# Signs of the expert weights on GpSimd, a new first-block order and an earlier far block in an attention and two-MLP kernel

## The chip, the cores and the metric

One core of one Trainium2 chip runs one launch. The metric is the device time in microseconds; before the change the median of three runs was 943.58 us (941.25 to 945.59).

## The reference, cut to what matters

Inputs are f32 (the weights reach the chip as 64-bit words, see below). Attention has 4 batches, 8 heads, 576 positions and head size 64. Heads 0 to 3 look back over 32 positions, heads 4 to 7 at positions of the same residue modulo 32. Then two MLPs over 2304 tokens follow:

```python
attn = softmax(where(mask, q @ k.T / 8, -1e9)) @ v      # per head
x = attn as (2304, 512)
h = x @ w_in;  x = (h - tanh(h)) @ w_out                # d_ff 2048
xn = x / sqrt(mean(x * x) + 1e-6) * rms_g
out = (silu(xn @ w_gate) * (xn @ w_val)) @ w_out        # d_ff 1536
```

## The kernel before, in words

Tokens are cut into nine sub-blocks of 256 (`subs`, numbered 0 to 8) and these into five groups, (0,1), (2,3), (4), (5,6), (7,8); group 2 is half as wide. The first MLP runs group by group, and in a group over 16 slices f of d_ff: `pe_h` makes h in 12 matmuls (three products of high and low fp32r parts, four chunks of 128), ScalarE takes the tanh (L680), VectorE subtracts and splits the result (L685, L696) with a ScalarE cast (L691) between, and `pe_x` adds 12 matmuls into four banks. The second MLP (from about 480 us) is TensorE work alone as far as the time goes.

A weight tile comes as 64-bit floats, 128 x 512 of them. `Weight.scale` (ScalarE L165, for the first five tiles GpSimd L167) scales the upper words into `ca`; `Weight.merge` builds the f32 on VectorE in three steps: L174 shifts `ca` left by three into `ct`, L175 puts the sign bit of `ca` in, L178 puts the top three bits of the lower words in. ScalarE casts to the high part (L185) and VectorE subtracts for the low part (L189). The 32 tiles of the first MLP are made this way while group 0 runs, two per slice f; the 36 tiles of the second MLP follow in the last group.

Attention of a sub-block is one `Local` object and, for the strided heads, a `Dense` one (sub-blocks 0 to 3, "near", and 6, "far") or `Strided` ones (4, 5, 7, 8). Local and Dense have four steps: `s` (score matmuls, then on VectorE the row maxima L298 or L301, on ScalarE the exp L312, on VectorE the sums and the scaling L320 to L322), `p` (TensorE transposes L331, ScalarE copies L335), `v` (matmuls with v) and the write-out to `xs` (L338, L342). Strided products are made by GpSimd (L504 for q and k, L537 for the probabilities and v) and reduced by VectorE (L509, L544).

What sets the order: the first block is written out by hand in the string `START` (s0L is step `s` of Local 0, m, e, n are its maxima, exp and scaling, A scale on GpSimd, B merge, P and Q the two parts, h a `pe_h`). After it a planner orders every engine's instructions, except that TensorE keeps the written order from group 1 on. During group g the attention of group g+1 is issued: `STINT[g]` lists the slices f before which its next s, p or v step is put (`pe_work`), and `work` spreads the strided items over slices. `EARLY = (5,)`: sub-block 5's strided scores are made in group 1 already.

Of the kernel before, what the change touches and what calls it, by code (L numbers as in the profile page):

```python
# [7 lines left out]
F32 = mybir.dt.float32  # L8
# [5 lines left out]
ALU = mybir.AluOpType  # L14
# [9 lines left out]
START = """  # L24
<tabcdwABwCDwww2ww
W9
s0Lx m0L0 s0Dx m0L1 m0D0 e0L0 m0D1 e0L1 n0L0 p0L0h0 A0 e0D0 n0L1 B0 p0L1h1 c0L0a s1Lx c0L1a e0D1 n0D0 v0Lh0
P0 n0D1 p0D0m0 y0L0 A1 p0D1m1 y0L1 z0L0 c0D0a z0L1 s1Dx c0D1a Q0 v0Dh1 m1L0 m1L1 y0D0 y0D1 z0D0 A2 e1L0 z0D1
m1D0 h0h0 e1L1 n1L0 m1D1 p1L0m0 T0 G0 c1L0a n1L1 I0 e1D0 J0 p1L1m1 B1 c1L1a e1D1 n1D0 P1 n1D1 p1D0m0 Q1
c1D0a p1D1m1 B2 v1Lm0 A3 c1D1a v1Dm1 y1L0 y1L1 z1L0 P2 h1h1 z1L1 y1D0 Q2 y1D1 z1D0 A4 X0 T1 z1D1 G1 h2h0 B3  # L30
# [5 lines left out]
def attn_moe_moe_kernel(  # L36
# [24 lines left out]
    nc = tc.nc  # L61
# [12 lines left out]
    groups = [(0, 1), (2, 3), (4,), (5, 6), (7, 8)]  # L74
    width = [SUB * len(g) for g in groups]
    NG = len(groups)
# [3 lines left out]
    def runs(s):  # L80

        r = []
        for i, (b, t) in enumerate(subs[s]):
            if r and r[-1][0] == b and r[-1][1] + r[-1][2] == t:
                r[-1][2] += 64
            else:
                r.append([b, t, 64, 64 * i])
        return r
# [3 lines left out]
    NEAR = 4  # L92

    SOON = {2: 6, 3: 2}
    STINT = {1: (5, 8, 11), 2: (1, 3, 4, 5, 7, 8, 10, 11, 13), 3: (1, 3, 5, 8, 10, 12)}
    GC = 2
    PR = 5 * 64
    LANES = (5, 7, 8)
    EARLY = (5,)
# [21 lines left out]
    for s in range(len(subs)):  # L121
        if len(runs(s)) > 1 or s in LANES:
            _, t0, n, _ = runs(s)[0]
# [25 lines left out]
    class Weight:  # L149
        def __init__(self, kind, f):  # L150
            self.kind, self.f = kind, f

        def load(self):
            kind, f = self.kind, self.f
            r = wts.tile([128, 4, 128], w_in.dtype, tag="w", name="raw")
            self.raw = r
            src = {"in": w_in, "gate": w_gate, "val": w_val, "out": w_out, "out2": w_out2}[kind]
            nc.sync.dma_start(out=r.rearrange("p c f -> p (c f)"), in_=src[f])

        def scale(self, eng):  # L160
            w = self.raw.rearrange("p c f -> p (c f)").bitcast(U32).rearrange("p (n t) -> p n t", t=2)
            self.lo, hi = w[:, :, 0], w[:, :, 1]
            self.a = cvt.tile([128, 512], F32, tag="ca", name="ca")
            if eng is nc.scalar:
                nc.scalar.mul(out=self.a, in_=hi.bitcast(F32), mul=2.0 ** -111)  # L165
            else:
                nc.gpsimd.tensor_scalar(  # L167
                    out=self.a, in0=hi.bitcast(F32), scalar1=2.0 ** -111, scalar2=1.0, op0=ALU.mult, op1=ALU.mult
                )

        def merge(self):
            a = self.a.bitcast(U32)
            t = cvt.tile([128, 512], U32, tag="ct", name="ct")
            nc.vector.tensor_scalar(out=t, in0=a, scalar1=3, scalar2=None, op0=ALU.logical_shift_left)  # L174
            nc.vector.scalar_tensor_tensor(  # L175
                out=t, in0=a, scalar=0x80000000, in1=t, op0=ALU.bitwise_and, op1=ALU.bitwise_or
            )
            nc.vector.scalar_tensor_tensor(  # L178
                out=t, in0=self.lo, scalar=29, in1=t, op0=ALU.logical_shift_right, op1=ALU.bitwise_or
            )  # L180
            self.b = t.bitcast(F32)
# [71 lines left out]
    class Heads:  # L253
# [35 lines left out]
        def st_m(self, i):  # L289

            w, ps = self.w, self.ps
            self.sm[i] = sm = self.room("sm", i, 4 * w).rearrange("q (h p t) -> q h p t", h=2, p=2)
            self.nm[i] = nm = att.tile([128, 2, 2], F32, tag="nm", name="nm", bufs=4)
            self.ss[i] = att.tile([128, 2, 2], F32, tag="ss", name="ss", bufs=4)
            m = dmask if w == 128 else mask if not self.near else add[96][:, i] if w == 96 else add[64]
            for hh in range(2):
                if self.early:
                    nc.vector.tensor_reduce(out=nm[:, hh], in_=ps[hh][:, i], axis=AX.X, op=ALU.max)  # L298
                else:
                    for p in range(2):  # L300
# [47 lines left out]
    class Local(Heads):  # L348
        w = 96
# [237 lines left out]
    loc = [Local(j) for j in range(len(subs))]  # L587
# [9 lines left out]
    class Work:  # L597


        def __init__(self, js):  # L600
            self.pe, self.st = [], []
            for j in js:
                kinds = [loc[j]]
                if isinstance(strd[j][0], Dense):
                    kinds += strd[j]
                else:
                    for o in strd[j]:
                        self.st += o.pvs if j in EARLY else o.items().qks + o.pvs
                    if j + 1 == EARLY[0]:
                        for o in (strd[i][0] for i in EARLY):  # L610
                            self.st += o.items().qks
                for nm, k in zip("spsvpv", (0, 0, 1, 0, 1, 1)):
                    if k < len(kinds):
                        self.pe.append(lambda o=kinds[k], nm=nm: self.stage(o, nm))

        @staticmethod
        def stage(o, nm):
# [42 lines left out]
    def new_x(g):  # L660
        if g < NG:
            xs[g] = mid.tile([128, 2, 4, 512], F32R, tag="xs", name="xs")
            for k, j in enumerate(groups[g]):
                xh[j] = xs[g][:, :, :, SUB * k:SUB * k + SUB]
# [182 lines left out]
    wks = [Work(groups[1])]  # L847
# [78 lines left out]
    for g, f, a, e in units:  # L926
        if g == 0:
            st1.to(2 * (f + 4))
        elif f == 0:
            if g == 1:  # L930
                order = ctx.enter_context(ExitStack())
                order.enter_context(tc.manual_schedule(engines={mybir.EngineType.PE}))
            if g == NG - 1:
                order.close()
            assert not wks[-1].pe and not wks[-1].st
            new_x(g + 1)
            if g + 1 < NG:
                wks.append(Work(groups[g + 1]))
        if g == NG - 1 and f == 0:
            poolT.close()  # L940
            pbx = ctx.enter_context(tc.tile_pool(name="pbx", bufs=1, side="right", reuse_waits="tile"))
            gcol = pbx.tile([128, 4], F32, name="gcol")
            nc.sync.dma_start(out=gcol, in_=rms_g.rearrange("(c p) -> p c", p=128))
            ones = pbx.tile([128, 128], F32R, name="ones")
            nc.vector.memset(ones.bitcast(F32), 1.0)
        rem = FA - 1 - f
        wk = wks[-1]

        def pe_work():
            if g in STINT:  # L950
                wk.run_pe(len(wk.pe) if f in STINT[g] else 0)
            elif f >= 2:
                wk.run_pe(max(rem, 1))

        def work():
            if f >= 6 or 0 < g < NG - 1:
                wk.run(wk.st, max(rem - SOON.get(g, 0), 1))

        unit(g, f, a, e, pe_work, work)
        if g == NG - 1:  # L960
            if f == 4:
                pg = prep(0, pbx)
            if pg is not None:
                next(pg, None)
# [127 lines left out]
```

## Time and profile before

| | us |
|---|---|
| median of the runs | 943.58 |
| the profiled execution | 945.39 |
| its span | 943.7 |
| TensorE busy | 911.2 |
| VectorE busy | 571.0 |
| ScalarE busy | 345.0 |
| GpSimd busy | 159.9 |

The span runs from the first to the last instruction; 1.7 us of the execution's time lie outside it. A view of stretches gives each engine's busy time and the granted TensorE clock in each, as a share of full speed. An instruction's row gives its start, its duration, and in brackets how long its engine had been idle and what ended that.

### The profile page before, as it was taken

The numbers are of one execution on the slowest core, as the hardware profiler recorded it, in microseconds if no ns is written. First come the engines' busy times: TensorE is split into PE (matmuls) and PEld (weight loads), VectorE is DVE, ScalarE is ACT, GpSimd is POOL, SyncE is SP. The second block draws the span as 40 slices with busy tenths as digits, with TensorE's granted clock in tenths as the row PEclk, the third lists the DMA queues.
The fourth block names the chain that finished last, engine by engine and source line by source line (L and its number), as shares of the span: only waits on it lengthen the run. The fifth ranks groups of instructions, "written<-read, shape, count | busy, mean of one in ns | idle before, by whom it ended". The sixth has DMA issues, their size and how long they took to land.

```text
span 943.7 us, 13656 instructions
## 1 busy us (share of the span) xinstructions
PE 911.2 (97%) x5251; PEld 756.8 (80%) x5251; DVE 571.0 (61%) x1263; ACT 345.0 (37%) x795; POOL 159.9 (17%) x216
## 2 busy tenths in 40 slices
PE   6799998999899999999999999999999999999998
PEld 4677876888799787888888888888888888888897
DVE  4899998987748979359999682262125312421212
ACT  4776743322453424256566332222111211111211
POOL 0100136784408686000000000000000000000000
PEclk8799998999999999999999999999999999999999
DMA  9845433311222110066444210101010001000100
GB/s 289 268 168 185 143 93 97 103 56 51 91 75 75 49 38 1 1 223 194 164 155 140 86 49 19 45 3 43 0 45 1 23 1 44 1 1 1 45 1 23
DMA packets 33729, 72.86 MB, mean 77 GB/s; under 512 B 6976, under 2 KB 15552, under 8 KB 33664
## 3 DMA queue, kind: packets, MB, share of 16 engines
q1 hardware_dynamic: 33664, 71.99, 23.5%
q8 instruction: 41, 0.67, 0.3%
q14 instruction: 24, 0.20, 0.1%
HBM read 62.54 MB, written 9.44 MB: 76 GB/s over the span
## 4 chain that ended last, share of the span: by engine, by line
PE 61%; DVE 2%; issue 0%; POOL 0%; DVEq 0%
PE ps_x L145 23%; PE ps_h L145 22%; PE ps_m L145 16%; DVE so L544 1%; DVE sm L301 0%; DVE g L696 0%; DVE tg L685 0%; PE ps_v L145 0%; DVE sm L322 0%; POOL pr L504 0%; DVE os L820 0%; POOL pr L537 0%; PE ps_p L331 0%; DVE pr L552 0%; DVE xs L563 0%
## 5 line engine op out<-in xcount | busy, mean ns | idle before, releaser
L145 PE MATMUL ps_x<-g,w 128*128 128x512 f32 (+1 forms) x984 | 221.0, 373 | 4.0 <-DVE w L189 2.1
L145 PE MATMUL ps_h<-xs,w 128*128 128x512 f32 (+1 forms) x984 | 214.4, 366 | 1.0 <-DVE xs L342 0.8
L145 PEld LDWEIGHTS ps_x<-g,w 128*128 128x128 f32 x984 | 171.3, 193 | 36.5 <-DVE w L189 3.0
L145 PEld LDWEIGHTS ps_h<-xs,w 128*128 128x128 f32 x984 | 170.6, 190 | 31.2 <-DVE xs L342 0.9
L795 DVE SCALAR_TENSOR_TENSOR s<-ps_m,s 128x512 f32<-128x512 f32 (+1 forms) x60 | 38.3, 638 | 222.9 <-PE ps_m L145 222.8
L145 PE MATMUL ps_h<-xn,w 128*128 128x512 f32 (+1 forms) x720 | 159.0, 369 | 0.0
L145 PE MATMUL ps_m<-xn,w 128*128 128x512 f32 (+1 forms) x720 | 158.4, 368 | 0.0
L145 PE MATMUL ps_x<-w,p 128*128 128x512 f32 x648 | 157.8, 391 | 0.0
L145 PEld LDWEIGHTS ps_h<-xn,w 128*128 128x128 f32 x720 | 126.8, 188 | 24.5
L145 PEld LDWEIGHTS ps_m<-xn,w 128*128 128x128 f32 x720 | 125.9, 188 | 23.1
L145 PEld LDWEIGHTS ps_x<-w,p 128*128 128x128 f32 x648 | 120.7, 188 | 25.6
L504 POOL TENSOR_TENSOR pr<-sk,sq 128x256 f32<-128x256 f32 (+2 forms) x101 | 83.1, 857 | 119.8 <-DMA sk<-in_k_str_dram 78.9
L794 ACT ACTIVATE s<-ps_h 128x512 f32<-128x512 f32 (+1 forms) x60 | 33.4, 556 | 163.9 <-PE ps_h L145 163.6
L537 POOL TENSOR_TENSOR pr<-sv,se 128x288 f32<-128x288 f32 (+12 forms) x104 | 72.0, 713 | 64.0 <-DVE so L544 19.7
L797 ACT CAST p<-s 128x512 fp32r<-128x512 f32 (+1 forms) x60 | 34.6, 577 | 122.4 <-DVE s L795 122.3
L691 ACT CAST g<-tg 128x512 fp32r<-128x512 f32 (+1 forms) x82 | 46.5, 568 | 86.2 <-DVE tg L685 85.7
L685 DVE SCALAR_TENSOR_TENSOR tg<-ps_h,tg 128x512 f32<-128x512 f32 (+1 forms) x82 | 50.6, 617 | 34.5 <-ACT tg L680 34.3
L680 ACT ACTIVATE tg<-ps_h 128x512 f32<-128x512 f32 (+1 forms) x82 | 44.4, 542 | 70.8 <-PE ps_h L145 70.4
L544 DVE TENSOR_REDUCE so<-pr 128x16 f32<-128x240 f32 (+11 forms) x104 | 64.3, 650 | 6.3 <-POOL pr L537 5.8
L696 DVE TENSOR_TENSOR g<-tg,g 128x512 fp32r<-128x512 f32 (+1 forms) x82 | 55.0, 670 | 10.2 <-ACT g L691 9.9
L798 DVE TENSOR_TENSOR p<-s,p 128x512 fp32r<-128x512 f32 (+1 forms) x60 | 38.2, 637 | 25.8 <-ACT p L797 25.6
L165 ACT ACTIVATE ca<-raw 128x512 f32<-128x512 f32 x63 | 41.9, 672 | 28.0 <-issue 8.0
(79 smaller groups left out, 674.6 us busy)
## 6 DMA issues: line engine op xcount, KB each, us to landing
raw<-in_w_out_dram SPq DMA_DIRECT2D x28, 512.0 KB, 5.2
raw<-in_w_in_dram SPq DMA_DIRECT2D x16, 512.0 KB, 7.8
raw<-in_w_gate_dram SPq DMA_DIRECT2D x12, 512.0 KB, 3.9
raw<-in_w_val_dram SPq DMA_DIRECT2D x12, 512.0 KB, 4.2
x2d<-xe SPq DMA_DIRECT2D x36, 128.0 KB, 1.8
x<-x2d SPq DMA_DIRECT2D x16, 256.0 KB, 3.9
out_dram<-o SPq DMA_DIRECT2D x16, 256.0 KB, 2.0
sk<-in_k_str_dram SPq DMA_DIRECT2D x4, 576.0 KB, 3.8
```

The source lines that it names most:

```text
L145: nc.tensor.matmul(out_, lhsT, rhs, start=start, stop=stop, skip_group_check=True)
L165: nc.scalar.mul(out=self.a, in_=hi.bitcast(F32), mul=2.0 ** -111)
L504: nc.gpsimd.tensor_tensor(out=pr, in0=self.k[:, a:e, :], in1=self.q[:, c - c0:c - c0 + 1, :].to_broadcast([128, e - a, D]), op=ALU.mult,)
L537: nc.gpsimd.tensor_tensor(out=pr, in0=self.v[:, 0:c + 1, a:e], in1=self.e[:, c - c0, 0:c + 1].unsqueeze(2).to_broadcast([128, c + 1, e - a ...
L544: pend.append(lambda: nc.vector.tensor_reduce(out=o[:, c - g0, a:e], in_=pr.rearrange("l c d -> l d c"), axis=AX.X, op=ALU.add))
L680: nc.scalar.activation(out=t, in_=h_of[g, f, a], func=ACTF.Tanh, scale=WS)
L685: nc.vector.scalar_tensor_tensor(out=t, in0=h_of.pop((g, f, a)), scalar=WS, in1=t, op0=ALU.mult, op1=ALU.subtract)
L691: nc.scalar.copy(out=t[:, 0], in_=t_of[g, f, a])
L696: nc.vector.tensor_tensor(out=t[:, 1], in0=t_of.pop((g, f, a)), in1=t[:, 0].bitcast(F32), op=ALU.subtract)
L795: nc.vector.scalar_tensor_tensor(out=s, in0=r[1], scalar=WS, in1=s, op0=ALU.mult, op1=ALU.mult)
L797: nc.scalar.copy(out=t[:, 0], in_=s)
L798: nc.vector.tensor_tensor(out=t[:, 1], in0=s, in1=t[:, 0].bitcast(F32), op=ALU.subtract)
```

## The change

Three things. The sign bit of the first MLP's 32 weight tiles is made by a new GpSimd instruction, which multiplies the upper words in place by 0.0 (a zero that keeps its sign); the merge is then two VectorE instructions instead of three. In `START` the Dense maxima, exps and the first merge stand later, and the s step of Local 1 after the v step of Local 0. And the first two steps (s and p) of Local 5 are issued at the end of group 1's list instead of the start of group 2's; `STINT` has five entries for group 1 and seven for group 2, and strided items are issued in group 1 from slice 3 on.

```diff
 START = """
-s0Lx m0L0 s0Dx m0L1 m0D0 e0L0 m0D1 e0L1 n0L0 p0L0h0 A0 e0D0 n0L1 B0 p0L1h1 c0L0a s1Lx c0L1a e0D1 n0D0 v0Lh0
+s0Lx m0L0 m0L1 e0L0 e0L1 n0L0 s0Dx p0L0h0 A0 n0L1 m0D0 m0D1 p0L1h1 c0L0a e0D0 e0D1 c0L1a B0 n0D0 v0Lh0 s1Lx
...
-    STINT = {1: (5, 8, 11), 2: (1, 3, 4, 5, 7, 8, 10, 11, 13), 3: (1, 3, 5, 8, 10, 12)}
+    STINT = {1: (4, 6, 8, 11, 14), 2: (2, 3, 6, 7, 9, 10, 13), 3: (1, 3, 5, 8, 10, 12)}
...
+            self.apart = kind in ("in", "out")
...
+            if self.apart:
+                nc.gpsimd.tensor_scalar(
+                    out=hi.bitcast(F32), in0=hi.bitcast(F32), scalar1=0.0, scalar2=1.0, op0=ALU.mult, op1=ALU.mult
+                )
...
-            nc.vector.tensor_scalar(out=t, in0=a, scalar1=3, scalar2=None, op0=ALU.logical_shift_left)
-            nc.vector.scalar_tensor_tensor(
-                out=t, in0=a, scalar=0x80000000, in1=t, op0=ALU.bitwise_and, op1=ALU.bitwise_or
-            )
+            if self.apart:
+                nc.vector.scalar_tensor_tensor(
+                    out=t, in0=a, scalar=3, in1=self.hi, op0=ALU.logical_shift_left, op1=ALU.bitwise_or
+                )
+            else:
...
-                for nm, k in zip("spsvpv", (0, 0, 1, 0, 1, 1)):
-                    if k < len(kinds):
+                for n, (nm, k) in enumerate(zip("spsvpv", (0, 0, 1, 0, 1, 1))):
+                    if k < len(kinds) and not (j in EARLY and n < 2):
...
+            for j in early:
+                for nm in "sp":
+                    self.pe.append(lambda o=loc[j], nm=nm: self.stage(o, nm))
...
-                wks.append(Work(groups[g + 1]))
+                wks.append(Work(groups[g + 1], EARLY if g == 1 else ()))
...
-            if f >= 6 or 0 < g < NG - 1:
+            if g > 1 or g == 1 and f >= 3:
```

The built programs differ at three places that matter below. First VectorE, around the last weight tiles of the first MLP; `w<-ct` is the last step of a tile, `so<-pr` and `sc_91<-pr` are reductions of strided products, `tg` and `g` belong to a slice's tanh. Before, up to the last `w<-ct`:

```order
L175 SCALAR_TENSOR_TENSOR ct<-ca,ct 128x512 x2
L544 TENSOR_REDUCE so<-pr 128x16
L189 TENSOR_TENSOR w<-ct,w 128x512
...
L685 SCALAR_TENSOR_TENSOR tg<-ps_h,tg 128x512
L178 SCALAR_TENSOR_TENSOR ct<-raw,ct 128x512
...
L509 TENSOR_REDUCE sc_91<-pr 128x4
L696 TENSOR_TENSOR g<-tg,g 128x512
L552 STREAM_TRANSPOSE pr<-so 128x128
L189 TENSOR_TENSOR w<-ct,w 128x512
```

After, the last two tiles (the second and the fifth row end them) and the rows behind:

```order
L189 SCALAR_TENSOR_TENSOR ct<-raw,ct 128x512
L200 TENSOR_TENSOR w<-ct,w 128x512
L530 TENSOR_REDUCE smx<-sc_91 128x2
L711 TENSOR_TENSOR g<-tg,g 128x512
L200 TENSOR_TENSOR w<-ct,w 128x512
L531 TENSOR_TENSOR se<-sc_91,smx 128x36
L700 SCALAR_TENSOR_TENSOR tg<-ps_h,tg 128x512
L535 TENSOR_REDUCE smx<-se 128x2
...
L555 TENSOR_REDUCE so<-pr 128x16 x6
```

Counted over the whole order, eight `so<-pr` reductions, one `sc_91<-pr` reduction, five tanh steps (three `tg`, two `g`), two `xs<-ps_v` and six small instructions that stood ahead of the last tile now stand behind it. The file's lines have shifted: L178 and L189 are now L189 and L200, L509 is L520, L524 is L535, L544 is L555, L685 and L696 are L700 and L711.

Second GpSimd, from its start; `raw<-raw` is the new instruction. Before:

```order
L167 TENSOR_SCALAR ca<-raw 128x512 x5
L504 TENSOR_TENSOR pr<-sk,sq 128x256 x3
L504 TENSOR_TENSOR pr<-sk,sq 128x320
```

After, the last rows of the first block and what follows:

```order
L169 TENSOR_SCALAR ca<-raw 128x512
L173 TENSOR_SCALAR raw<-raw 128x512 x27
L515 TENSOR_TENSOR pr<-sk,sq 128x256 x3
L515 TENSOR_TENSOR pr<-sk,sq 128x320
L515 TENSOR_TENSOR pr<-sk,sq 128x256
L173 TENSOR_SCALAR raw<-raw 128x512
```

The 32 new instructions stand in front of the strided products, the last of them behind five of these.

Third TensorE, where group 1 ends and group 2 begins (128x256 is group 2); `ps_s<-lq` is step s of a Local, `ps_p` step p. Before:

```order
L145 MATMUL ps_x<-g,w 128x512 x24
L145 MATMUL ps_h<-xs,w 128x256 x12
L145 MATMUL ps_x<-g,w 128x512 x12
...
L145 MATMUL ps_s<-lq 64x96 x16
L145 MATMUL ps_h<-xs,w 128x256 x12
L145 MATMUL ps_x<-g,w 128x256 x12
...
L331 MATMUL ps_p<-tab,sm 96x128 x8
```

After:

```order
L145 MATMUL ps_s<-lq 64x96 x16
L145 MATMUL ps_x<-g,w 128x512 x12
L145 MATMUL ps_h<-xs,w 128x512 x12
...
L342 MATMUL ps_p<-tab,sm 96x128 x8
...
L145 MATMUL ps_h<-xs,w 128x256 x24
L145 MATMUL ps_v<-pT,v 64x64 x16
```

Step s of Local 5 stands six half slices (of 512 columns) ahead of its step p, inside group 1; before, three half slices of 256 columns lay between them. The s and p steps of Local 4 have moved from slices 5 and 8 to slices 4 and 6.

## Rows read from the trace of the kernel before

**Rows 1.** The page: busy times; VectorE in 40 slices; the scale's group (busy us, mean ns).
```profile
PE 911.2 (97%) x5251; PEld 756.8 (80%) x5251; DVE 571.0 (61%) x1263; ACT 345.0 (37%) x795; POOL 159.9 (17%) x216
...
DVE  4899998987748979359999682262125312421212
...
L165 ACT ACTIVATE ca<-raw 128x512 f32<-128x512 f32 x63 | 41.9, 672 | 28.0 <-issue 8.0
```
**Rows 2.** The chain that ended last, one piece (start, us, what).
```profile
413.18 2.72 PE ps_x L145 x12
```
**Rows 3.** Stretches: us, busy PE, PEld, DVE, ACT, POOL, then clock, DMA share, GB/s.
```profile
37.00:60.00 23.00, 20.50 (x176) 17.72 (x175) 21.65 (x69) 16.73 (x51) 0.00 (x0) 0.93 0.39 147
...
123.00:164.00 41.00, 35.33 (x188) 26.26 (x188) 37.02 (x78) 18.00 (x33) 19.64 (x24) 0.88 0.33 100
```
**Rows 4.** TensorE in order of time, 37 to 59 us and 124 to 163 us.
```profile
36.98 1.70 PE L145 MATMUL ps_h<-xs,w 128*128 128x256 f32 x12
...
49.27 1.06 PE L331 MATMUL ps_p<-tab,sm 128*96 128x128 f32 x4 [2.50 <-DVE ss L321]
...
59.10 4.45 PE L145 MATMUL ps_x<-g,w 128*128 128x512 f32 x24
...
123.83 0.41 PE L145 MATMUL ps_v<-pT,dv 64*32 64x64 f32 x4
...
151.82 5.56 PE L145 MATMUL ps_x<-g,w 128*128 128x512 f32 x11 [1.05 <-DVE w L189]
...
163.23 2.88 PE L145 MATMUL ps_x<-g,w 128*128 128x512 f32 x12
```
**Rows 5.** VectorE, the last tile's last step, in order of time.
```profile
150.64 1.12 DVE L189 TENSOR_TENSOR w<-ct,w 128x512 fp32r<-128x512 f32 x1
```
**Rows 6.** VectorE groups from 37 to 114 us (busy us, mean ns, idle before).
```profile
L189 DVE TENSOR_TENSOR w<-ct,w 128x512 fp32r<-128x512 f32 x22 | 14.6, 684 | 1.2 <-ACT w L185 1.2
L174 DVE TENSOR_SCALAR ct<-ca 128x512 uint32<-128x512 uint32 x23 | 9.0, 419 | 0.0
```
**Rows 7.** The same from 114 to 152 us, where GpSimd works beside them.
```profile
L189 DVE TENSOR_TENSOR w<-ct,w 128x512 fp32r<-128x512 f32 x8 | 6.5, 816 | 0.0
...
L174 DVE TENSOR_SCALAR ct<-ca 128x512 uint32<-128x512 uint32 x6 | 3.5, 590 | 0.0
...
L544 DVE TENSOR_REDUCE so<-pr 128x16 f32<-128x272 f32 x4 | 2.5, 631 | 0.0
```
**Rows 8.** GpSimd and VectorE in order of time, 23 to 33 us.
```profile
23.30 0.65 POOL L167 TENSOR_SCALAR ca<-raw 128x512 f32<-128x512 f32 x1 [2.97 <-DMA raw<-in_w_out_dram]
30.46 1.09 POOL L167 TENSOR_SCALAR ca<-raw 128x512 f32<-128x512 f32 x1 [6.51 <-DVE ct L175]
...
30.35 0.69 DVE L178 SCALAR_TENSOR_TENSOR ct<-raw,ct 128x512 uint32<-128x512 uint32 x1
30.96 0.61 DVE L320 TENSOR_SCALAR ss<-ss 128x4 f32<-128x4 f32 x1
...
32.16 0.16 DVE L320 TENSOR_SCALAR ss<-ss 128x4 f32<-128x4 f32 x1
```
**Rows 9.** TensorE in order of time where group 2 begins.
```profile
248.40 0.89 PE L145 MATMUL ps_s<-lq 64*64 64x96 f32 x32
...
250.75 1.60 PE L145 MATMUL ps_x<-g,w 128*128 128x256 f32 x12
252.19 1.60 PE L145 MATMUL ps_h<-xs,w 128*128 128x256 f32 x12
256.90 0.61 PE L331 MATMUL ps_p<-tab,sm 128*96 128x128 f32 x4 [3.12 <-DVE ss L320]
...
261.19 1.59 PE L145 MATMUL ps_h<-xs,w 128*128 128x256 f32 x12
```
**Rows 10.** TensorE in order of time, the first block.
```profile
9.71 0.69 PE L145 MATMUL ps_s<-dq 64*64 64x64 f32 x32 [3.13 <-DMA dq<-in_near_d_dram]
12.76 1.94 PE L331 MATMUL ps_p<-tab,sm 128*96 128x128 f32 x8 [2.36 <-ACT sm L312]
```

More of the change, by code (lines that the diff above doesn't have):

```diff
@@ L161, in scale @@
             w = self.raw.rearrange("p c f -> p (c f)").bitcast(U32).rearrange("p (n t) -> p n t", t=2)
-            self.lo, hi = w[:, :, 0], w[:, :, 1]
+            self.lo, self.hi = w[:, :, 0], w[:, :, 1]
+            hi = self.hi
             self.a = cvt.tile([128, 512], F32, tag="ca", name="ca")
@@ L173, in merge @@
             t = cvt.tile([128, 512], U32, tag="ct", name="ct")
-            nc.vector.tensor_scalar(out=t, in0=a, scalar1=3, scalar2=None, op0=ALU.logical_shift_left)
-            nc.vector.scalar_tensor_tensor(
-                out=t, in0=a, scalar=0x80000000, in1=t, op0=ALU.bitwise_and, op1=ALU.bitwise_or
-            )
+            if self.apart:
[3 more added lines that the diff above has]
+            else:
+                nc.vector.tensor_scalar(out=t, in0=a, scalar1=3, scalar2=None, op0=ALU.logical_shift_left)
+                nc.vector.scalar_tensor_tensor(
+                    out=t, in0=a, scalar=0x80000000, in1=t, op0=ALU.bitwise_and, op1=ALU.bitwise_or
+                )
             nc.vector.scalar_tensor_tensor(
@@ L597, in attn_moe_moe_kernel, with __init__ @@
     class Work:
-        def __init__(self, js):
+        def __init__(self, js, early=()):
             self.pe, self.st = [], []
```

## The prediction, made before the changed kernel was run

> **What bounds the kernel now.** The page first: TensorE is busy for 97% of the span, and VectorE stands near full until about 180 us and is far from it in the second half [rows 1]. From about 400 us TensorE works without a gap in the chain of waits, twelve 512-column matmuls in 2.72 us, 0.227 us each [rows 2]. So a gain can only come from the first 400 us, and what is gained there shifts the rest of the program forward one to one. Next, the stretches: between 37 and 60 us, and between 123 and 164 us, TensorE idles (23.0 less 20.5 us, and 41.0 less 35.3) and the clock averages 0.93 and 0.88, so it runs partly on the lower of its two levels, 1.2 instead of 2.4 GHz, after the gaps; VectorE is busy for 94 and 90% of them [rows 3].
>
> How much is lost there I take from TensorE's rows in order of time against the full-speed price. A 256-column matmul costs 0.120 us (twelve in 252.19 - 250.75 = 1.44 us [rows 9]). From 36.98 to 59.10 us the order holds 72 of 256 columns and 24 of 512, 8.6 + 5.4 us, and 2.3 us of attention matmuls by the same reading: 16.3 us of work in 22.1, **5.8 us lost**. From 123.83 to 163.23 it holds 112 of 512, 25.4 us, and 1.5 us of attention: 26.9 us in 39.4, **12.5 us lost** [rows 4]. Both times the idle rows name VectorE; the last wait of the second stretch is for the last step of the last weight tile, a step that ends at 150.64 + 1.12 = 151.76, and TensorE goes on at 151.82 [rows 4, 5]. A third loss is where group 2 begins: from 252.19 to 261.19 there are 24 matmuls of 256 columns and the eight transposes, 3.7 us of work in 9.0, **5.3 us lost**, first 3.12 us of waiting for VectorE's softmax sums [rows 9]. Together 23.6 us.
>
> **The change part by part.**
>
> *First block.* The local maxima and sums no longer wait behind the Dense scores, whose data arrive at 9.71 us; the transposes that start at 12.76 us could start 2.36 us earlier [rows 10]. Against that the first merge now waits for two GpSimd instructions in place of one (0.65 us for the second, as long as a scale that nothing blocks [rows 8]), the Dense scaling stands behind it on VectorE, and on TensorE s of Local 1 stands behind the v step, which waits for ScalarE. Bounds -2.4 and +1.0 us; I take **0**, since the path ends at `pe_h` of the first slice, which needs the Dense half, not the local one, and that has won nothing.
>
> *The weight tiles.* VectorE bounds the stretch from 37 to 151.8 us, so its work ahead of the last tile's last step is to be counted. Removed: the shift, 28 times after 37 us (the first four lie before). It lasts 0.419 us [rows 6], and neighbours overlap by 0.08 (0.69 us from 30.35, the next starts at 30.96 [rows 8]), but an instruction that needs its result starts later; at 0.36 us a step, -10.1 us. Moved behind the last tile, by the order: eight `so<-pr` at 0.63 - 0.08 us [rows 7], 4.4; five tanh steps at 0.68 - 0.08 (as long as L189 [rows 6]), 3.0; nine short ones, estimated from their kinds at 1.7: -9.1 us. The new merge step reads two SBUF tiles like L175, so I give it the 0.69 us of L178, which reads two as well [rows 8].
>
> Added on GpSimd: 32 sign instructions of some 0.65 us, 21 us on an engine that has five scales before 37 us and then nothing until the strided products (0.00 us from 37 to 60 [rows 3]). Its own time is covered. But it isn't free for VectorE. At 30.46 us a scale was issued while L178 ran, and it lasted 1.09 instead of 0.65 us; the small L320 behind L178 lasted 0.61 instead of 0.16 us and both ended at 31.55 to 31.57 [rows 8]. So the two engines took turns: GpSimd waited for L178 to end at 31.04, then ran for 0.5 us, and VectorE waited those 0.45 us. Where GpSimd is busy L189 lasts 816 instead of 684 ns and the shift 590 instead of 419 [rows 6, 7]. Nearly every VectorE instruction of a tile is of such a kind; the tanh subtraction (PSUM input) and reductions are not. A sign instruction costs VectorE nothing to 0.52 us; I take 0.36, 0.45 in four cases of five: 28 x 0.36 = +10.1 us. **By itself the new merge thus gains nothing; the moved rows do.** The products of GpSimd beside the last tiles lose about one more microsecond of such turns (eight L189 at 0.13, six shifts at 0.17, half of it). Sum for VectorE: -10.1 - 9.1 + 10.1 - 1 = -10.1, the last tile at about 141.7 instead of 151.8 us. TensorE waits for it, so 10 of the 18.3 us lost in the two stretches return: **-10** (bounds -18.3, if the turns cost nothing, and -5.6, at 0.52 each, 14.6 us in all).
>
> The Trainium skill, "SBUF — State Buffer", section "Who interferes with whom", has a rule against this change: VectorE instructions with two SBUF inputs and GpSimd instructions that read SBUF share a port pair, and the one that comes second is blocked for the whole instruction of the other. The 0.45 us that L320 waited agree; by the rule the sum would stand at its bad end, 934 us, which is the first rival below.
>
> *Behind it.* The strided products start no later (their keys are loaded when the fourth Dense block's scores are done), and in group 1 VectorE has lost the weights, so the moved rows find room there. The new chain of waiting is data, scale, sign, merge; ScalarE's next scale waits for a free `ca`, of which there are two. One tile per 2.72 us (two per slice of 24 matmuls) against 0.67 (L165 [rows 1]) + 0.65 + 0.69 us for that loop leaves it slack.
>
> *Group 2's beginning.* The steps s and p of Local 5 now lie in group 1, six half slices of 2.72 us apart, where 4.3 us of work had lain between them (252.19 + 1.44 less 249.29, the end of s [rows 9]). The 5.3 us go, and the next s, of Local 6, has six half slices of 256 columns, 8.6 us, in which to come. Local 4's steps are now four half slices apart, 10.9 us, with VectorE busy on strided products: bounds -5.3 (nothing new) and 0 (the same wait again). I take **-5** here, and **+1** for a new short wait in group 1.
>
> Sum: 0 - 10 - 5 + 1 = -14 us on 945.39 us, 931.4. The profiled execution lies 1.8 us above the median of the runs, 943.58; against the median it is 929.6, and I say **930 us**.
>
> **The rivals.** (1) Full blocking: each sign costs VectorE 0.52 us, the tile stage returns 5.6 us, the sum is -9.6: 934 us. For it: the turns in [rows 8]; against: the tanh rows and maxima let GpSimd through. (2) GpSimd fits into the gaps, VectorE stops being the bound, all 23.6 us return: 920 us. For it: 21 us of GpSimd in over 100 us; against: VectorE has hardly a gap there. (3) The stage doesn't move: its end is set by another wait, such as the merges' in-order place behind a sign that comes late, or the attention chain on TensorE; only group 2's beginning counts, -4: 939.6 us. For it: the wait at 49.27 us is for softmax sums, not for a weight; against: the last wait is for the last tile [rows 4, 5]. (4) **Slower**: the sign reads and writes every second word in place, where the scale writes a full row, and if that doubles the 0.52 us, 28 x 1.04 = 29 us go to VectorE against 20.2 won there; the last tile is 9 us later, less the 4 us of group 2: 948.6 us and more, since the clock falls longer. From 0.86 us per sign the change loses. Against it: the strided read alone costs the scale no more than 0.65 us, and nothing in the trace shows an instruction in place.
>
> **How the numbers follow.** Forecast 0.40, rivals (1) 0.20, (2) 0.20, (3) 0.13, (4) 0.07. About 0.5%, 4.7 us, can be told from no change. Faster by more holds the forecast, (1), (2): 0.80, of which I give 0.02 to the middle, 0.78; same is (3) with that, 0.15; slower 0.07. The range runs from a microsecond below rival (2) to a little above rival (3), 919 to 941 us: it takes in both bounds of the tile term and leaves out (4) and some 0.12 in the tails of the others.
>
> **What would show it.** In the profile after: VectorE's group for the merge has two rows of about 0.69 us; GpSimd has 32 sign rows, many of about 1.0 us (blocked) and few of 0.65; L200 (the old L189) and small rows behind them are longer than 684 and 160 ns while no strided product runs; the last tile ends near 142 us; the clock of 123 to 164 us is above 0.95; no wait of 3 us stands where the 256-column matmuls begin. The prediction is wrong if L200 keeps 684 ns (rival 2), if sign rows hold the port for about 1 us (rival 4), or if the idle time in front of the last tile is as long as before though the tile ends earlier (rival 3).

## The result, and the profile after

The changed kernel takes **937.15 us** (median of 5 runs, 936.82 to 937.85) beside 944.12 us for the kernel before in the same comparison: ratio 0.9915, 95% interval 0.9894 to 0.9936. A second comparison gave 0.990 (0.9875 to 0.9925). It is faster by 0.9%, 7.0 us, where 13.6 were forecast. The spans of the two profiled executions differ by 7.8 us (943.7 and 935.9).

First the page of the changed kernel, as [rows 1]: busy times, then VectorE in 40 slices.

```profile
PE 911.1 (97%) x5251; PEld 758.2 (81%) x5251; DVE 567.8 (61%) x1231; ACT 345.6 (37%) x795; POOL 187.1 (20%) x248
...
DVE  4799997988868988179999672272126312421211
```

VectorE has 32 instructions fewer and only 3.2 us less to do; GpSimd has 32 more and 27 us more. Much of the step that left VectorE in each tile came back as longer rows there. These are its groups from 37 to 145 us (busy us, mean ns, idle before), and GpSimd's sign from 0 to 145 us. Before, from 37 to 114 us, a tile's shift took 419 ns and its low part 684 [rows 6], and the two steps between them:

```profile
L175 DVE SCALAR_TENSOR_TENSOR ct<-ca,ct 128x512 uint32<-128x512 uint32 x23 | 15.2, 683 | 0.0
L178 DVE SCALAR_TENSOR_TENSOR ct<-raw,ct 128x512 uint32<-128x512 uint32 x23 | 15.2, 684 | 0.0
```

After (the sum of a tile falls from 2470 to 2320 ns):

```profile
L189 DVE SCALAR_TENSOR_TENSOR ct<-raw,ct 128x512 uint32<-128x512 uint32 x29 | 23.5, 827 | 0.1
L200 DVE TENSOR_TENSOR w<-ct,w 128x512 fp32r<-128x512 f32 x30 | 21.8, 739 | 0.4 <-ACT w L196 0.3
L181 DVE SCALAR_TENSOR_TENSOR ct<-ca,raw 128x512 uint32<-128x512 uint32 x29 | 21.6, 754 | 0.5 <-POOL raw L173 0.5
```
```profile
L173 POOL TENSOR_SCALAR raw<-raw 128x512 f32<-128x512 f32 x32 | 29.7, 937 | 62.3 <-ACT ca L167 56.4 <-issue 3.1 <-DMA lq<-in_q_loc_dram 2.4
```

One collision in order of time, GpSimd and then VectorE: two signs in 1.78 us, and beside them two low-word merges in 1.75. The two L200 rows that follow, which are as long as merges when nothing blocks them (685 and 692 ns a row in a run below), take 1.29.

```profile
61.68 1.78 POOL L173 TENSOR_SCALAR raw<-raw 128x512 f32<-128x512 f32 x2 [3.26 <-ACT ca L167]
```
```profile
62.26 1.75 DVE L189 SCALAR_TENSOR_TENSOR ct<-raw,ct 128x512 uint32<-128x512 uint32 x2
63.92 0.68 DVE L711 TENSOR_TENSOR g<-tg,g 128x512 fp32r<-128x512 f32 x1
64.54 1.29 DVE L200 TENSOR_TENSOR w<-ct,w 128x512 fp32r<-128x512 f32 x2
```

The last step of the last tile answers to [rows 5]: it ends at 139.40 + 0.68 = 140.08 us, before at 151.76.

```profile
139.40 0.68 DVE L200 TENSOR_TENSOR w<-ct,w 128x512 fp32r<-128x512 f32 x1
```

The stretches of [rows 3], with the same columns:

```profile
37.00:60.00 23.00, 20.75 (x171) 18.49 (x162) 19.36 (x50) 14.02 (x38) 4.09 (x5) 0.83 0.58 227
60.00:123.00 63.00, 63.00 (x444) 50.64 (x442) 61.60 (x144) 46.04 (x112) 21.91 (x22) 1.00 0.45 148
123.00:164.00 41.00, 38.03 (x245) 30.25 (x245) 35.45 (x72) 17.33 (x37) 20.53 (x25) 0.96 0.33 108
```

Between 123 and 164 us TensorE idles for 3.0 us instead of 5.7, at a mean clock of 0.96 instead of 0.88. VectorE is still full from 60 to 123 us. Before, only part of that idle time was for a weight (`w`): 2.3 of the 5.6 us in its waits. The rest was for a tanh slice (`g`) and for an attention write-out (`xs`). Beside the 1.05 us in [rows 4] these were its longest waits:

```profile
127.63 1.02 PE L331 MATMUL ps_p<-tab,sm 128*64 128x128 f32 x4 [1.65 <-DVE xs L342]
...
146.54 2.12 PE L145 MATMUL ps_x<-g,w 128*128 128x512 f32 x8 [1.01 <-DVE w L189]
150.27 0.49 PE L145 MATMUL ps_x<-g,w 128*128 128x512 f32 x1 [1.61 <-ACT g L691]
```

After, TensorE in order of time shows the waits that are left or new, answering to [rows 4] and, from 251 us on, to [rows 9]. Between 60 and 250 us there are two, 2.60 us for a `g` and 0.37 us for an `xs`; none is for a weight:

```profile
37.59 2.93 PE L145 MATMUL ps_h<-xs,w 128*128 128x256 f32 x12
...
42.23 1.60 PE L145 MATMUL ps_h<-xs,w 128*128 128x256 f32 x12
...
51.29 0.76 PE L342 MATMUL ps_p<-tab,sm 128*96 128x128 f32 x4 [2.25 <-DVE ss L331]
...
128.90 1.91 PE L145 MATMUL ps_x<-g,w 128*128 128x512 f32 x6 [2.60 <-ACT g L706]
...
251.31 0.38 PE L145 MATMUL ps_s<-lq 64*64 64x96 f32 x2
254.05 0.89 PE L145 MATMUL ps_s<-lq 64*64 64x96 f32 x30 [2.37 <-DVE xs L353]
...
317.06 0.61 PE L342 MATMUL ps_p<-tab,sm 128*96 128x128 f32 x4 [1.93 <-DVE sm L333]
317.43 4.58 PE L145 MATMUL ps_x<-g,w 128*128 128x512 f32 x12
```

At 128.90 us, where the granted clock then is 0.72 up to 135 us, TensorE waits for a slice's `g`: ScalarE's tanh (L695) started at 123.65, but VectorE got to the tanh step at 126.80, behind softmax sums, a merge and two strided sums:

```profile
123.26 1.22 DVE L181 SCALAR_TENSOR_TENSOR ct<-ca,raw 128x512 uint32<-128x512 uint32 x1
124.41 0.70 DVE L331 TENSOR_SCALAR ss<-ss 128x4 f32<-128x4 f32 x1
125.03 0.41 DVE L520 TENSOR_REDUCE sc<-pr 128x4 f32<-128x256 f32 x1
...
125.72 0.68 DVE L189 SCALAR_TENSOR_TENSOR ct<-raw,ct 128x512 uint32<-128x512 uint32 x1
...
126.80 0.66 DVE L700 SCALAR_TENSOR_TENSOR tg<-ps_h,tg 128x512 f32<-128x512 f32 x1
```

Some of these rows are longer than alone (1.22 us for 0.68, 0.70 for 0.16). No sign runs beside them; GpSimd's strided products do:

```profile
122.76 5.05 POOL L515 TENSOR_TENSOR pr<-sk,sq 128x256 f32<-128x256 f32 x5
```

At 254 us the scores of Local 6 wait for the bank of Local 5's v, whose write-out (L353) stands on VectorE behind the strided products (L555):

```profile
250.82 1.07 DVE L555 TENSOR_REDUCE so<-pr 128x16 f32<-128x256 f32 x2
...
252.15 0.56 DVE L555 TENSOR_REDUCE so<-pr 128x16 f32<-128x256 f32 x1
252.63 0.41 DVE L353 TENSOR_TENSOR xs<-ps_v,xs 128x256 fp32r<-128x256 f32 x1
...
253.48 0.42 DVE L353 TENSOR_TENSOR xs<-ps_v,xs 128x256 fp32r<-128x256 f32 x1 [0.22 <-ACT xs L349]
```

To see where the time went, TensorE's position at four points of the order (starts in us, each in its profiled execution; "from 3 to 2" is the time from the first point to the second):

| kernel | s of Local 3 | last tile ends | group 2's first h | group 3's first h | span | from 3 to 2 | group 2 |
|---|---|---|---|---|---|---|---|
| before | 91.92 | 151.76 | 242.70 | 305.45 | 943.7 | 150.8 | 62.8 |
| after | 93.91 | 140.08 | 240.02 | 298.35 | 935.9 | 146.1 | 58.3 |
| sign twice | 93.66 | 145.80 | 245.36 | 306.45 | 942.5 | 151.7 | 61.1 |
| sign on ScalarE | 94.55 | 134.03 | 237.41 | 298.26 | 936.0 | 142.9 | 60.9 |
| Local 6 later | 92.38 | 138.29 | 238.23 | 293.68 | 931.4 | 145.9 | 55.5 |

Since Local 5's scores and transposes, 1.6 us of TensorE (0.83 and 0.79 by the rows of the same steps of Locals 6 and 7 further down), moved from group 2 to group 1, 1.6 us is taken off "from 3 to 2" and put on "group 2" for a comparison with before. So the 7.8 us are: start +2.0, weight stage and group 1 -6.3, group 2 -2.8, the rest -0.7. Of the 6.3 some 2.7 are idle time of TensorE; the rest goes with the clock of the stretch from 123 to 164 us.

### The profile page after: what moved, and what is told of

Same layout as the page of the kernel before. It is cut to its first block, busy times and chain, and to the rows that moved or that the text cites. A ratio compares the mean times of both kernels' runs of the same rounds, so it can differ in the third digit from the quotient of the medians.

```text
span 935.9 us, 13698 instructions
## 1 busy us (share of the span) xinstructions
PE 911.1 (97%) x5251; PEld 758.2 (81%) x5251; DVE 567.8 (61%) x1231; ACT 345.6 (37%) x795; POOL 187.1 (20%) x248
## 4 chain that ended last, share of the span: by engine, by line
PE 73%; DVE 9%; POOL 4%; issue 1%; ACT 1%; DMA 0%; SPq 0%; DVEq 0%; POOLq 0%; ACTq 0%
PE ps_x L145 28%; PE ps_h L145 28%; PE ps_m L145 16%; POOL pr L515 3%; DVE so L555 3%; DVE g L711 1%; DVE tg L700 1%; DVE ct L181 1%; DVE sc L520 1%; POOL pr L548 1%; DVE w L200 0%; DMA sq<-in_q_str_dram 0%; PE ps_p L342 0%; DVE ct L189 0%; DVE sm L312 0%
## 5 line engine op out<-in xcount | busy, mean ns | idle before, releaser
L548 POOL TENSOR_TENSOR pr<-sv,se 128x288 f32<-128x288 f32 (+12 forms) x104 | 69.2, 687 | 60.8 <-DVE so L555 19.8
L695 ACT ACTIVATE tg<-ps_h 128x512 f32<-128x512 f32 (+1 forms) x82 | 44.5, 542 | 70.1 <-PE ps_h L145 69.9
L555 DVE TENSOR_REDUCE so<-pr 128x16 f32<-128x272 f32 (+11 forms) x104 | 64.9, 650 | 8.1 <-POOL pr L548 7.7
L700 DVE SCALAR_TENSOR_TENSOR tg<-ps_h,tg 128x512 f32<-128x512 f32 (+1 forms) x82 | 50.5, 616 | 27.8 <-ACT tg L695 27.7
L711 DVE TENSOR_TENSOR g<-tg,g 128x512 fp32r<-128x512 f32 (+1 forms) x82 | 55.7, 680 | 9.7 <-ACT g L706 9.1
```

The costliest lines, as they stand in the source:

```text
L548: nc.gpsimd.tensor_tensor(out=pr, in0=self.v[:, 0:c + 1, a:e], in1=self.e[:, c - c0, 0:c + 1].unsqueeze(2).to_broadcast([128, c + 1, e - a ...
L555: pend.append(lambda: nc.vector.tensor_reduce(out=o[:, c - g0, a:e], in_=pr.rearrange("l c d -> l d c"), axis=AX.X, op=ALU.add))
L695: nc.scalar.activation(out=t, in_=h_of[g, f, a], func=ACTF.Tanh, scale=WS)
L700: nc.vector.scalar_tensor_tensor(out=t, in0=h_of.pop((g, f, a)), scalar=WS, in1=t, op0=ALU.mult, op1=ALU.subtract)
L711: nc.vector.tensor_tensor(out=t[:, 1], in0=t_of.pop((g, f, a)), in1=t[:, 0].bitcast(F32), op=ALU.subtract)
```

## The experiments

**The parts, each alone, and all but one.** The theory at this point: the gain of the weight stage hangs on the sign (the shorter merge lets the order put strided products behind the last tile), group 2's beginning gives about 3 us, and the first block nothing or a small loss.

Sign and merge alone, as a diff to the changed kernel (the block's row, the table and the far block's early steps are put back):
```
-s0Lx m0L0 m0L1 e0L0 e0L1 n0L0 s0Dx p0L0h0 A0 n0L1 m0D0 m0D1 p0L1h1 c0L0a e0D0 e0D1 c0L1a B0 n0D0 v0Lh0 s1Lx
+s0Lx m0L0 s0Dx m0L1 m0D0 e0L0 m0D1 e0L1 n0L0 p0L0h0 A0 e0D0 n0L1 B0 p0L1h1 c0L0a s1Lx c0L1a e0D1 n0D0 v0Lh0
...
-    STINT = {1: (4, 6, 8, 11, 14), 2: (2, 3, 6, 7, 9, 10, 13), 3: (1, 3, 5, 8, 10, 12)}
+    STINT = {1: (5, 8, 11), 2: (1, 3, 4, 5, 7, 8, 10, 11, 13), 3: (1, 3, 5, 8, 10, 12)}
...
-                wks.append(Work(groups[g + 1], EARLY if g == 1 else ()))
+                wks.append(Work(groups[g + 1]))
```


> The change's sign and merge alone; first block, groups' table and far block as before. Theory: the gain of the weight stage hangs on this part alone, since the two-step merge is what lets the order put eight products and three tanh steps behind the last tile: last tile near 140 us, loss of TensorE between 123 and 164 us about 6.7 us smaller than before, about 937 us. Rival: the sign's turns give back what the merge saves, and the stage's gain came from the first block's new order: 943 to 945 us.

Measured: 939.54 us, ratio 0.9925 (0.9901 to 0.9949), -7.1 us at 945 us. The stage's gain does hang on the sign: the last tile ends at 137.97 us, and "from 3 to 2" takes 145.1 us instead of 150.8. But TensorE then waits longer where group 2 begins (for Local 5's sums, 4.26 us; before 3.12 [rows 9]).

The first block alone (to the kernel before):
```
-s0Lx m0L0 s0Dx m0L1 m0D0 e0L0 m0D1 e0L1 n0L0 p0L0h0 A0 e0D0 n0L1 B0 p0L1h1 c0L0a s1Lx c0L1a e0D1 n0D0 v0Lh0
+s0Lx m0L0 m0L1 e0L0 e0L1 n0L0 s0Dx p0L0h0 A0 n0L1 m0D0 m0D1 p0L1h1 c0L0a e0D0 e0D1 c0L1a B0 n0D0 v0Lh0 s1Lx
```


> The first block's new order alone, merge in three steps. Theory: it costs 0 to 2 us, because TensorE is 0.6 us later at the start of the second slice and 1.7 us later at 60 us in the changed kernel: 944 to 946 us. Rival: the local scores ahead of the Dense ones gain up to 2.4 us: 941.7 us.

Measured: 943.41 us, ratio 0.9971 (0.9957 to 0.9985): the rival, a gain of about 2.7 us. Its profile is not ahead at s of Local 3 (92.59 against 91.92); it gains behind that point, to group 2's first h in 148.2 instead of 150.8 us, with the last tile at 148.98: seven products instead of eight lie ahead of it.

Group 2's beginning alone (to the kernel before; the constructor of `Work` as in the change):
```
-    STINT = {1: (5, 8, 11), 2: (1, 3, 4, 5, 7, 8, 10, 11, 13), 3: (1, 3, 5, 8, 10, 12)}
+    STINT = {1: (4, 6, 8, 11, 14), 2: (2, 3, 6, 7, 9, 10, 13), 3: (1, 3, 5, 8, 10, 12)}
...
-                wks.append(Work(groups[g + 1]))
+                wks.append(Work(groups[g + 1], EARLY if g == 1 else ()))
...
-            if f >= 6 or 0 < g < NG - 1:
+            if g > 1 or g == 1 and f >= 3:
```


> The far block's scores and transposes in group 1, with the new tables, alone; merge and first block as before. Theory: the 5.3 us lost where group 2 begins are replaced by a wait of 2.4 us for VectorE's write-out of Local 5, so -3 us: about 941 us. Rival A: all 5.3 us return, 939 us. Rival B: the wait in group 3 that got longer in the changed kernel eats the gain: 944 us.

Measured: 942.01 us, ratio 0.9963 (0.9943 to 0.9984), -3.5 us. The theory holds in its time; a wait of 1.69 us for the same write-out of Local 5 stands there.

All but the first block's order (to the changed kernel):
```
-s0Lx m0L0 m0L1 e0L0 e0L1 n0L0 s0Dx p0L0h0 A0 n0L1 m0D0 m0D1 p0L1h1 c0L0a e0D0 e0D1 c0L1a B0 n0D0 v0Lh0 s1Lx
+s0Lx m0L0 s0Dx m0L1 m0D0 e0L0 m0D1 e0L1 n0L0 p0L0h0 A0 e0D0 n0L1 B0 p0L1h1 c0L0a s1Lx c0L1a e0D1 n0D0 v0Lh0
```


> The changed kernel with the first block's order of before. Theory: the first block's new order costs 0.6 to 2 us, so this is faster than the changed kernel by as much: 935 to 936.5 us. Rival: the new order pays: 938 us or more.

Measured: 935.32 us, ratio 0.9886 (0.9866 to 0.9906). The parts add up without the block (0.75 + 0.37% for 1.14%); with it they don't: it gains 0.3% alone and none, or a loss of that size, in the sign's company. The intervals touch, so its part there stays unsettled here.

**What holds the weight stage.** Sign on ScalarE. This kernel leaves out the sign of the weights (presumably ScalarE's product with zero doesn't keep it), so it shows times alone:
```
-                nc.gpsimd.tensor_scalar(
-                    out=hi.bitcast(F32), in0=hi.bitcast(F32), scalar1=0.0, scalar2=1.0, op0=ALU.mult, op1=ALU.mult
-                )
+                nc.scalar.mul(out=hi.bitcast(F32), in_=hi.bitcast(F32), mul=0.0)
```


> The changed kernel with the sign made by ScalarE (times zero) in place of GpSimd; order of VectorE up to the last tile nearly the same. Theory: GpSimd's turns at the port cost VectorE about 0.31 us a sign, so without them the 29 low-word merges fall from 827 to about 690 ns and the last tile comes near 131 us in place of 140; TensorE gains what the tile's wait still holds, 2 to 5 us, less what ScalarE's 21 us of extra work delays: 932 to 937 us. Rival: the merges stay near 800 ns (the in-place sign's data, not the port, slow them), last tile near 140 us: 937 us or slower.

Measured: 937.54 us, ratio 0.9929 (0.9908 to 0.995): the time of the rival, by the mechanism of the theory. It can't be told from the changed kernel in time. Here are VectorE's groups and the stretches of this run:

```profile
L198 DVE TENSOR_TENSOR w<-ct,w 128x512 fp32r<-128x512 f32 x30 | 20.7, 692 | 2.7 <-ACT w L194 2.6
L179 DVE SCALAR_TENSOR_TENSOR ct<-ca,raw 128x512 uint32<-128x512 uint32 x29 | 19.7, 686 | 0.1
L187 DVE SCALAR_TENSOR_TENSOR ct<-raw,ct 128x512 uint32<-128x512 uint32 x29 | 19.6, 685 | 0.1
```
```profile
60.00:123.00 63.00, 63.00 (x453) 50.41 (x452) 59.45 (x151) 58.42 (x140) 1.29 (x2) 1.00 0.45 148
123.00:164.00 41.00, 41.00 (x270) 33.33 (x269) 32.37 (x70) 16.82 (x32) 21.14 (x28) 1.00 0.32 97
```

Without GpSimd's turns the three rows of a tile fall to 686, 685 and 692 ns, 257 ns less together, and TensorE doesn't idle between 60 and 164 us (it waits 1.77 us at 222.78, for a tanh step). The tile is 6 us earlier and TensorE gains 3.2 us up to group 2 (142.9 against 146.1); VectorE's order isn't the same in this kernel, so the row means are surer here than the place of the tile. At group 2 most of it is taken back: Local 5's write-out hangs on the strided products, the wait grows, and the matmuls behind it take longer (2.47 us where twelve of 256 columns take 1.44): from 252.50 to 256.30 us the granted clock is 0.58, part of the stretch on the lower level, 1.2 GHz.

```profile
252.50 1.55 PE L145 MATMUL ps_s<-lq 64*64 64x96 f32 x30 [3.08 <-DVE xs L351]
253.99 2.47 PE L145 MATMUL ps_x<-g,w 128*128 128x256 f32 x12
```

The sign issued twice (the second finds a zero with its sign and leaves it):
```
                 nc.gpsimd.tensor_scalar(
                     out=hi.bitcast(F32), in0=hi.bitcast(F32), scalar1=0.0, scalar2=1.0, op0=ALU.mult, op1=ALU.mult
                 )
+                nc.gpsimd.tensor_scalar(
+                    out=hi.bitcast(F32), in0=hi.bitcast(F32), scalar1=0.0, scalar2=1.0, op0=ALU.mult, op1=ALU.mult
+                )
```


> The changed kernel with each sign instruction issued twice, so that GpSimd's turns double and VectorE's own work stays. Theory: VectorE loses another 0.31 us a sign, 9 us in 28 tiles: last tile near 149 us, time 943 to 946 us. Rival: the second sign runs beside instructions that don't need the port, or VectorE's stage isn't what TensorE waits for: 937 to 939 us.

Measured: 943.53 us, ratio 0.999 (0.9977 to 1.0004): the whole gain is gone. VectorE's order is nearly that of the change; its rows are longer:

```profile
L192 DVE SCALAR_TENSOR_TENSOR ct<-raw,ct 128x512 uint32<-128x512 uint32 x29 | 25.1, 881 | 0.1
L203 DVE TENSOR_TENSOR w<-ct,w 128x512 fp32r<-128x512 f32 x29 | 24.9, 868 | 0.1
L184 DVE SCALAR_TENSOR_TENSOR ct<-ca,raw 128x512 uint32<-128x512 uint32 x29 | 22.2, 774 | 0.1
```

The second sign adds 0.20 us a tile in these rows, 5.9 us in 29; counted from s of Local 3, TensorE reaches group 2 5.6 us later. On this side VectorE's time goes to TensorE nearly one to one, and again not through a weight: TensorE idles 7.7 us on the way, all of it for tanh slices and write-outs, this the longest:

```profile
134.15 1.66 PE L145 MATMUL ps_x<-g,w 128*128 128x512 f32 x6 [2.61 <-ACT g L709]
```

The late tanh step ahead of the sums (in group 0 the tanh step is also written ahead of the attention step, and the load of the next block's q and k moves with the sums):
```
+                if o is strd[3][0]:
+                    held.append([2, o])
+                    return
...
+                o = held.pop()[1]
+                with tc.issue_after(ins.ins):
+                    for i in range(2):
+                        o.st_n(i)
...
+        if g == 0:
+            dve_g(g, f, a, e)
         pe_work()
-        dve_g(g, f, a, e)
+        if g > 0:
+            dve_g(g, f, a, e)
```


> The changed kernel with the softmax sums of the fourth Dense block issued on VectorE behind the tanh step of the slice that TensorE waited for at 128.9 us, instead of ahead of it. Theory: the stage is held by this tanh step, not by the last tile: the wait of 2.60 us at 128.9 us and the half-clock matmuls behind it go, 3 to 4 us: 933 to 934.5 us. Rival: the last tile, or the transposes that the sums feed, wait in its place: 936.5 to 938 us.

Measured: 935.65 us, ratio 0.9911 (0.9886 to 0.9935), not to be told from the change: the rival. The wait falls from 2.60 to 0.58 us, and two others come behind it:

```profile
123.95 2.11 PE L145 MATMUL ps_x<-g,w 128*128 128x512 f32 x8 [0.58 <-ACT g L725]
...
130.10 0.60 PE L342 MATMUL ps_p<-tab,sm 128*64 128x128 f32 x4 [0.64 <-DVE sm L333]
...
132.81 4.19 PE L145 MATMUL ps_h<-xs,w 128*128 128x512 f32 x11 [1.88 <-DVE tg L710]
```

So this late row alone doesn't hold the stage; with VectorE full, moving it ahead made others late.

**Group 2's beginning, repaired.** The scores of Local 6 one slice later:
```
-    STINT = {1: (4, 6, 8, 11, 14), 2: (2, 3, 6, 7, 9, 10, 13), 3: (1, 3, 5, 8, 10, 12)}
+    STINT = {1: (4, 6, 8, 11, 14), 2: (2, 4, 6, 7, 9, 10, 13), 3: (1, 3, 5, 8, 10, 12)}
```


> The changed kernel with the scores of Local 6 one slice later in group 2 (table entry 3 becomes 4). Theory: they waited 2.37 us at 254 us for VectorE's write-out of Local 5, which stands behind strided products; one slice of 2.9 us later the bank is free: about 934.8 us. Rival: the write-out holds the next use all the same, or Local 6's transposes now wait for its sums: 936.5 to 938 us.

Measured: 932.97 us, ratio 0.9872 (0.9849 to 0.9895). From group 2's first h to group 3's it takes 55.5 us, 5.7 less than before after the 1.6 us: about what was forecast for this term. By the timed runs the interval just touches that of the changed kernel; the profiles are clearer, since the three later kernels with this entry take 55.5 to 55.7 us there, and the changed kernel in its second profile 59.8. TensorE there:

```profile
250.87 1.60 PE L145 MATMUL ps_h<-xs,w 128*128 128x256 f32 x12
252.39 0.89 PE L145 MATMUL ps_s<-lq 64*64 64x96 f32 x32
253.22 1.69 PE L145 MATMUL ps_x<-g,w 128*128 128x256 f32 x12
```

The last four ran in one comparison, the first of them the changed kernel itself.

> The changed kernel itself, as the reference for the three others of this call on the same chip. All theories: about 0.9915 of before, 936.5 us.

Measured: 936.6 us, ratio 0.990 (0.9875 to 0.9925).

Also the transposes of Local 7 one slice later, and with them its v step (5 becomes 6):
```
-    STINT = {1: (4, 6, 8, 11, 14), 2: (2, 4, 6, 7, 9, 10, 13), 3: (1, 3, 5, 8, 10, 12)}
+    STINT = {1: (4, 6, 8, 11, 14), 2: (2, 4, 6, 7, 9, 10, 13), 3: (1, 4, 6, 8, 10, 12)}
```


> The changed kernel with the scores of Local 6 one slice later (3 becomes 4) and also the transposes of Local 7 one slice later (3 becomes 4). Theory: the wait of 1.93 us in group 3 for Local 7's softmax, with the half-clock matmuls behind it, goes too, 2 to 3 us on top of the 4 us that the first entry gave: about 930 us. Rival: Local 7's later steps or the strided chain wait in its place: 932.5 us as with the first entry alone.

Measured: 931.57 us, ratio 0.9847 (0.9821 to 0.9874). The wait of 1.93 us is gone, and the twelve matmuls behind it take 2.8 us to the next row's start and not 4.4; Local 8 waits later instead, 0.49 and 0.81 us at 350 us. The intervals of this run and the one before overlap, so the second entry's own worth, some 2 us by the ratios, isn't certain.

```profile
313.99 1.04 PE L342 MATMUL ps_p<-tab,sm 128*96 128x128 f32 x8
314.78 2.98 PE L145 MATMUL ps_x<-g,w 128*128 128x512 f32 x12
...
350.57 0.61 PE L342 MATMUL ps_p<-tab,sm 128*96 128x128 f32 x4 [0.49 <-DVE ss L332]
```

Both entries, with the first block in the order of before (to the kernel of the run above):
```
-s0Lx m0L0 m0L1 e0L0 e0L1 n0L0 s0Dx p0L0h0 A0 n0L1 m0D0 m0D1 p0L1h1 c0L0a e0D0 e0D1 c0L1a B0 n0D0 v0Lh0 s1Lx
+s0Lx m0L0 s0Dx m0L1 m0D0 e0L0 m0D1 e0L1 n0L0 p0L0h0 A0 e0D0 n0L1 B0 p0L1h1 c0L0a s1Lx c0L1a e0D1 n0D0 v0Lh0
```


> The same two entries, and the first block in its order of before. Theory: in the sign's company the new order of the first block costs 1 to 3 us, so this is faster than the run with the two entries alone by as much: 927 to 929 us. Rival: the new order is worth 2.7 us as it was by itself, so this is slower by that: 932 to 933 us. If they agree within 1 us, the block's order can't be told from nothing.

Measured: 930.06 us, ratio 0.9838 (0.981 to 0.9867), the fastest of all kernels here. Beside the run above it is 1.5 us faster by the medians, with intervals that overlap: the block's order can't be told from nothing.

Both entries, the first block of the change, and the edit of the late tanh step (its diff stands above):
```
-    STINT = {1: (4, 6, 8, 11, 14), 2: (2, 3, 6, 7, 9, 10, 13), 3: (1, 3, 5, 8, 10, 12)}
+    STINT = {1: (4, 6, 8, 11, 14), 2: (2, 4, 6, 7, 9, 10, 13), 3: (1, 4, 6, 8, 10, 12)}
...
+                if o is strd[3][0]:
+                    held.append([2, o])
```


> The two entries, and the sums of the fourth Dense block behind the tanh step that was late. Theory: the time won in the weight stage is no longer taken by the wait where group 2 begins, so the 1.5 us that the moved sums gave at first, or more, come on top: 927 to 929 us. Rival: the wait for the tanh step is only replaced by the waits behind it (1.88 us at 132.8 us in the first run of this edit): as with the two entries alone, within 1 us.

Measured: 930.28 us, ratio 0.984 (0.9813 to 0.9867): 1.3 us, inside the intervals too. The rival stands.

## Why the prediction was right in direction and twice too large

*Right.* The new merge gained little by itself, as forecast: VectorE's busy time fell by 3.2 us in the whole run. The turns at the port are real: rows of GpSimd and VectorE lengthen together, and a tile's rows are short again without the sign on GpSimd (686, 685, 692 ns a row without, 754, 827, 739 with it). The last tile was put at 141.7 us and ended at 140.08. That it came so near is partly luck: with the price of a sign as measured the same sum gives 138.9, and this execution was 2.0 us behind at s of Local 3. The clock of 123 to 164 us was put at over 0.95 and is 0.96. Nothing behind group 1 waited for weights, and Local 4's and Local 5's steps in group 1 found room: the "+1 for a new short wait" wasn't needed.

*The price of a sign* was taken as 0.36 us; a tile's three rows show 0.26 (257 ns against the sign on ScalarE) for the first sign and 0.20 for a second. The count was nearly right: by the rows 29 shifts, and not 28, lie after 37 us, 0.4 us. The Trainium skill, "SBUF — State Buffer", section "Who interferes with whom", lets the second of the two be blocked for the whole instruction. Single rows agree (two merges in 1.75 instead of 1.29 us), but as a sum per tile, rival (1) with 0.52 us is double what was measured, probably because part of each sign falls beside VectorE rows that don't need the port; no run separates this.

*The step that failed first* is "TensorE waits for it, so 10 of the 18.3 us lost in the two stretches return", where "it" is the last tile. The last tile came 11.7 us earlier, but the second stretch returned 6.3 us and the first nearly nothing: from its second `ps_h` row (39.96 us before, 42.23 after) to s of Local 3 TensorE took 52.0 us before and 51.7 after, as its wait there, for softmax sums, went from 2.50 to 2.25 us. In the second stretch only 2.3 of the 5.6 us of waits before were for weights; the prediction had taken the last wait for all of them. Afterwards no wait is for a weight, and 2.60 us are for a tanh step.

The sum had credited all 9.1 us of rows that the order moved behind the last tile. Moved is not removed: of them 3.0 us were tanh steps, and those TensorE needs as well, tile or no tile. With only the eight strided products (4.4 us) counted and the turns at 0.26 (28 of them, 7.3 us), the same sum gives -10.1 - 4.4 + 7.3 - 1 = -8.2, nearer to the 6.3 measured; that split is worked out, not measured by itself. What the runs do show is that TensorE waits for whatever stands late in VectorE's queue, and not for the last tile: twice the sign makes group 2 5.6 us later for 5.9 us of VectorE with no wait for a weight; without GpSimd's turns TensorE stops idling from 60 to 164 us; and a single late tanh step put ahead gains nothing. Rival (3), an end "set by another wait", was half right.

*The second step* is "The 5.3 us go, and the next s, of Local 6, has six half slices of 256 columns, 8.6 us, in which to come". It counted how long Local 6's own softmax has, and not what its scores need before they start: the bank of Local 5's v, one slice earlier, whose write-out is queued on VectorE behind the strided products. A wait of 2.37 us took the place of the one removed, and 2.8 us were won instead of 5. One entry of the table moved by one slice wins the rest, as shown: 5.7 us. The price was about right and the place was missed. Where group 2 begins, a wait also takes back what is won ahead of it: with the sign on ScalarE TensorE comes 2.6 us earlier and Local 5's write-out only 1.6, so that 2.37 become 3.08 us; with the sign alone, in the old order, the wait for Local 5's sums grows from 3.12 to 4.26.

*The first block*, taken as 0, was +2.0 us in the pair of profiles, but this can't be put down to the order: with the same block and the same sign, s of Local 3 starts between 90.62 and 93.91 us in five other profiles and this one, and with the old block and the sign between 90.38 and 92.78 in three. By the timed runs its part lies between a gain of 0.3% alone and none or a small loss beside the sign. What follows group 2 gave 0.7 us.

## What to carry to other kernels

An order that moves rows behind a milestone makes the milestone early; the waiting engine can gain only by those rows that it doesn't itself wait for. List every wait of a stretch by what ended it, and count the full engine's whole load between two points, not the one row that ends last. When a stage is moved to an earlier place, look at what its successor reuses, the PSUM bank above all, and at what stands on the releasing engine ahead of the release. Giving work to GpSimd beside a full VectorE is paid in VectorE's time, here 0.20 to 0.26 us for an instruction of 0.65: measure it by issuing it twice or by moving it to another engine.

## What was not expected of the hardware

The start isn't repeatable to the microsecond. The first Dense block's scores start between 6.19 and 10.05 us in the profiles, in all but the earliest after a wait for their data, and the mean granted clock of the first 37 us lies between 0.71 and 0.79. The same twelve matmuls behind the same attention steps took 1.70 us in [rows 4] and 2.93 in the changed kernel; the stretch behind their start was granted the full clock there and 0.59 here, as this row of the changed kernel shows:

```profile
37.60:42.20 4.60, 4.60 (x28) 4.60 (x25) 2.57 (x6) 2.04 (x5) 0.00 (x0) 0.59 0.69 270
```

Nor does every idle stretch cost clock. After the 1.93 us at 317 us the next stretch had 0.66, and after the 2.37 us at 254 us none was lost:

```profile
255.00:265.00 10.00, 10.00 (x85) 10.00 (x86) 5.48 (x28) 5.59 (x23) 0.00 (x0) 1.00 0.23 59
317.00:322.00 5.00, 4.94 (x17) 4.04 (x18) 4.91 (x11) 1.50 (x3) 5.00 (x7) 0.66 0.24 65
```

The duration of a blocked GpSimd instruction says little of its price: a sign lasts 0.64 us at the least, 0.94 on average and 3.47 at the most, and costs VectorE 0.20 to 0.26 on average.
